# A linear-attention recurrence in half chunks of 64 tokens, stacked on the partitions

## The chip, the cores and the metric

The kernel runs on one NeuronCore of a Trainium2 chip. The metric is the device time of one execution in microseconds; the kernel before took 582.66 us (median of 3 runs, 580.79 to 582.68). The execution that was profiled took 582.26 us, of which the profile's span, from the first to the last instruction, is 580.3 us. All data are fp32 on the chip; the two weight matrices arrive as 64-bit floats and are converted there.

## What is computed

The reference is a gated linear recurrence (RWKV6, "Finch") followed by a two-layer block with a hard-swish gate. Cut to what matters:

```python
# r, k, v, w: (B=4, H=8, S=768, D=48); u: (H, D)
for t in range(S):
    cur = einsum('bhd,bhe->bhde', u * k[t], v[t])
    y[t] = einsum('bhd,bhde->bhe', r[t], state + cur)
    state = w[t][..., None] * state + einsum('bhd,bhe->bhde', k[t], v[t])
x = y.transpose(0, 2, 1, 3).reshape(3072, 384)
h = x @ w_in                       # 384 x 2048
out = (h * clip(h + 3, 0, 6) / 6) @ w_out   # 2048 x 384
```

For a piece of the sequence the recurrence becomes matrix products. With the decays multiplied up along the piece, r and k are scaled (called R and K below). The products K^T R, masked to the part above the diagonal, are the weights with which earlier tokens of the piece enter later ones; u gives the diagonal; the state from before the piece is read with R; and K^T v, added to the decayed state, is the next state.

## The kernel before, in words

**Tiling.** The 3072 tokens are 24 chunks of L = 128. Two sequences run side by side: chunks i and i+1 belong to different sequences, and chunk i continues chunk i-2. Chunks 0, 1, 12 and 13 are the first of their sequences. Eight heads of 48 are four pairs (P = 4): one head of a pair (g = 0) lies on partitions 0 to 47, the other (g = 1) on 64 to 111. Four chunks make a block of 512 tokens (BC = 4), which goes through the two big matrix products; there are six blocks (NB = 6).

**Steps of a chunk**, with the function and its engine:

- back_scan and fore_scan (L355, L364, VectorE) multiply the decays up along the tokens, backwards into E and forwards into W; make_k and make_r (L375, L379) scale k in place in E and r in place in W. They run on VectorE for chunks below EARLY, later on GpSimd. least (L382, ScalarE) saves the chunk's whole decay.
- own and own_sum give the diagonal u·r·k. For chunks below BY_PE it is one product on VectorE (L388) and four small matmuls (own_dot, L398); later two products on GpSimd from r and k laid out by token (L391, L392) and a reduction on VectorE (L406). diagonal (L414, ScalarE) spreads it over A, eight copies of the identity scaled by one column each.
- score (L422): for each pair two matmuls of 48 rows, 128 columns of weights and 128 moving columns, on the upper and the lower half of the array's rows. above (L429, VectorE) puts the part above the diagonal into A.
- turn_k (L438) and turned_k (L443): K turned so that tokens lie on the partitions.
- read: read_state (L474) multiplies the decayed state S with R; write (L484) computes K^T v; read_values (L491) multiplies v with A. State and values add up in one PSUM tile, y_ps. leave (L544, L545, ScalarE) copies it out into xT and, for the last pair of heads, into x3; last_pair moves x3 into xT by DMA.
- new_state (L448, L450, VectorE) adds the decayed state and K^T v; decay (L455) multiplies the state by the next chunk's whole decay.

In block 0 the last pair of heads can't wait for the DMA: read_last, leave_last and read_rest spread it by a matmul with a selection matrix (L521).

**Block work.** Block 0 uses the plain products (up L577, down L596) for its first half and the seven-product scheme for the rest; blocks 1 to 5 use that scheme throughout, which forms two-by-two products with seven instead of eight multiplications (up_product L678, down_product L729, with sums on VectorE and evacuation on ScalarE and VectorE).

**Order.** Nothing is ordered by hand. plan.add gives each step an engine, an estimate of its length, what it comes after, a due time (the key) and the buffers it holds; Plan.order walks through them and emits, for each engine, the step with the lowest key among those that can start. Each engine then runs its list in order. The due times of the recurrence follow from BASE (when a block starts) minus LAG; START, CONV, UP and SUMS are due times of the first stage, in which the weights are converted (fetch, low, whole, shift, join, full). Up to the first up product, spare time on TensorE is filled with matmuls on the identity (spin, L1047; ten of them are sets of four small ones, L1044).

Of the kernel before, what the change touches and what calls it, by code (L numbers as in the profile page):

```python
# [18 lines left out]
L = 128  # L19
GP = 64  # L20
# [6 lines left out]
LAG = 12.5  # L27
BEHIND = (-1, -1, -1, 0, 6, 7)
BY_PE = 4
OWN = 0.5  # L30
EARLY = 3
START = (-119.6, -152.0, -58.6, -43.4, 14.5, 25.8)
CONV = (-91.7, 6.6)
UP = (-83.9, 4.3, -71.3, 4.8)
SUMS = (53.5, 2.3)
# [148 lines left out]
def fast_path(tc, feat, tok, wflat, ub, ug, moe_w_in, moe_w_out, out, flag, n_chunks):  # L184
# [3 lines left out]

    nc = tc.nc
# [15 lines left out]
    with ExitStack() as ctx:  # L205
# [24 lines left out]
        mask = const.tile([128, L], U8, name="mask")  # L230
        back = const.tile([PR, P, L + 1], F32, name="back")
        starts = [const.tile([PR, P, L + 1], F32, name=f"start_{i}") for i in range(2)]
# [6 lines left out]
        def constants():  # L239

            nc.vector.memset(back, 0.0)
            nc.vector.memset(back[:, :, L:], 1.0)
            for b in starts:
# [3 lines left out]
            make_identity(nc, ident)  # L247

            mask_f = wk.tile([128, L], F32, name="clip")
            nc.gpsimd.memset(mask_f, 1.0)  # L250
            nc.gpsimd.affine_select(out=mask_f, in_=mask_f, compare_op=ALU.is_gt, fill=0.0, base=0,
                                    pattern=[[1, L]], channel_multiplier=-1)
            nc.gpsimd.tensor_copy(out=mask, in_=mask_f)

            x3_0 = blocks[0]["x3"] = wk.tile([PR, MB], F32, name="x3", bufs=1)
# [6 lines left out]


        n = P * L
        plan.ring("feat", 3)
        plan.ring("tok", 3)

        def load_feat(i):
            a = io.tile([PR, nf], F32, name="feat_in")
            if i == 0:  # L270
                nc.sync.dma_start(out=a[:, 2 * n:], in_=feat[chunk_of[i], :, 2 * n:])
                nc.scalar.dma_start(out=u_col, in_=ug)
            else:
                nc.sync.dma_start(out=a, in_=feat[chunk_of[i]])
            st[i].update(a=a, r=a[:, :n].rearrange("q (p t) -> q p t", p=P),
                         k=a[:, n:2 * n].rearrange("q (p t) -> q p t", p=P), w=a[:, 2 * n:])
# [7 lines left out]
        def load_tok(i):  # L284
            b = io.tile([L, 3, HD], F32, name="tok_in", bufs=3)
            if i < BY_PE:
                nc.sync.dma_start(out=b[:, 2], in_=tok[chunk_of[i], :, 2])
            else:
                nc.sync.dma_start(out=b.rearrange("s c e -> s (c e)"), in_=tok[chunk_of[i]].rearrange("s c e -> s (c e)"))
            st[i].update(rt=b[:, 0], kt=b[:, 1], v=b[:, 2].rearrange("s (h d) -> s h d", d=D))  # L290
# [55 lines left out]
        for r, k in (("E", 2), ("W", 2), ("rk", 1), ("dg", 2), ("A", 2), ("kn", 2), ("S", 2), ("x", 2), ("x3", 1), ("y", 1),  # L346
# [3 lines left out]
        w_min = const.tile([PR, NT, P], F32, name="w_min")  # L350

        def back_scan(i):
            d = st[i]
            E_ = wk.tile([PR, P * (L + 1)], F32, name="E", bufs=2)
# [3 lines left out]
            d["E"] = E_.rearrange("q (p t) -> q p t", p=P)  # L358
            nc.vector.reciprocal(out=starts[i % 2][:, :, 0:1], in_=d["E"][:, :, 0:1])

        def fore_scan(i):
            d = st[i]
            W_ = wk.tile([PR, P * (L + 1)], F32, name="W", bufs=2)
# [3 lines left out]
            d["R"] = W_.rearrange("q (p t) -> q p t", p=P)[:, :, :L]  # L367
# [4 lines left out]
        def make_k(i):  # L372
            d = st[i]
            d["K"] = d["E"][:, :, 1:]
            early(i).tensor_mul(d["K"], d["k"], d["K"])  # L375
# [8 lines left out]
        def own(i):  # L384
            d = st[i]
            if i < BY_PE:
                d["rk"] = wk.tile([PR, P, L], F32, name="rk", bufs=1)
                nc.vector.tensor_mul(d["rk"], d["r"], d["k"])  # L388
# [20 lines left out]
        def diagonal(i, x):  # L409
            d = st[i]  # L410
            if x == 0:
                d["A"] = wk.tile([L, H, L], F32, name="A")
            for h in range(x * H // 2, (x + 1) * H // 2):
                nc.scalar.activation(out=d["A"][:, h, :], in_=ident, func=ACT.Copy, scale=d["dg"][:, h])  # L414

        def score(i):
            d = st[i]
            d["a_ps"] = [pp.tile([128, P, L], F32, name="bankB"), pp.tile([128, P, L], F32, name="bankC", bufs=2)]
            for p in range(P):
                for g in range(2):  # L420
                    rows = slice(g * GP, g * GP + D)
                    nc.tensor.matmul(d["a_ps"][g][:, p, :], lhsT=d["K"][rows, p, :], rhs=d["R"][rows, p, :],  # L422
                                     start=True, stop=True)

        def above(i):

            d = st[i]
            for g in range(2):
                nc.vector.copy_predicated(  # L429
                    out=d["A"].rearrange("s (p g) t -> s g p t", g=2)[:, g],  # L430
                    mask=mask.rearrange("s (x t) -> s x t", x=1).to_broadcast([L, P, L]),
                    data=d["a_ps"][g])

        def turn_k(i):
            d = st[i]
            d["kn_ps"] = pp.tile([L, P, PR], F32, name="ps")
            for p in range(P):
                nc.tensor.transpose(d["kn_ps"][:, p, :], d["K"][:, p, :], ident[0:PR, 0:PR])  # L438

        def turned_k(i):  # L440
            d = st[i]
            d["kn"] = wk.tile([L, P, PR], F32, name="kn")
            nc.scalar.copy(out=d["kn"], in_=d["kn_ps"])  # L443

        def new_state(i):
            d = st[i]
            if is_first(i):
                nc.vector.tensor_copy(out=states[i % 2], in_=d["kv_ps"])  # L448
            else:
                nc.vector.tensor_add(states[i % 2], d["S"], d["kv_ps"])  # L450

        def decay(i):
            d = st[i]
            d["S"] = wk.tile([PR, P, D], F32, name="S")
            early(i).tensor_mul(d["S"], states[i % 2], d["E"][:, :, 0:1].to_broadcast([PR, P, D]))  # L455


        PLACES = ((0, 0), (0, 3), (1, 2), (1, 0))

        def into(i, p, g):  # L460
            d = st[i]
            bank, at = PLACES[p]
            rows = (g ^ bank) * GP
            fresh = (bank, rows) not in d["started"]
            d["started"].add((bank, rows))
            return dict(out=d["y_ps"][rows:rows + D, bank, at, :], start=fresh, skip_group_check=True)
# [919 lines left out]
```

## Time and profile before

| What | Value |
|---|---|
| Time, median of 3 | 582.66 us |
| Span of the profiled execution | 580.3 us |
| DVE (VectorE) busy | 408.7 us, 70% |
| ACT (ScalarE) busy | 265.7 us, 46% |
| POOL (GpSimd) busy | 120.4 us, 21% |
| First up product of block 0 (L577) starts | 31.01 us |
| First up product of block 1 (L678) starts | 147.60 us |
| Moved by DMA | 65.70 MB, mean 113 GB/s |

How to read it: the profile names the engines PE (TensorE matmuls), PEld (TensorE weight loads), DVE, ACT, POOL and SP (the queue that issues transfers). The page has the busy time of each, the same in 40 slices of the span, the DMA queues, the chain of waits that ended last (followed backwards from the last instruction, each step to what released it), the groups of instructions by source line, and the transfers. Besides the page, the trace answers questions: busy time by stretch, a timeline, who waited for whom. A matmul in fp32 shows as two records[...], with a weight load ahead of each.

### The profile page before, as it was taken

The numbers are of one execution on the slowest core, as the hardware profiler recorded it, in microseconds if no ns is written. First come the engines' busy times: TensorE is split into PE (matmuls) and PEld (weight loads), VectorE is DVE, ScalarE is ACT, GpSimd is POOL, SyncE is SP. The second block draws the span as 40 slices with busy tenths as digits, with TensorE's granted clock in tenths as the row PEclk, the third lists the DMA queues.
The fourth block names the chain that finished last, engine by engine and source line by source line (L and its number), as shares of the span: only waits on it lengthen the run. The fifth ranks groups of instructions, "written<-read, shape, count | busy, mean of one in ns | idle before, by whom it ended". The sixth has DMA issues, their size and how long they took to land.

```text
span 580.3 us, 10344 instructions
## 1 busy us (share of the span) xinstructions
PE 568.5 (98%) x4064; PEld 505.4 (87%) x4064; DVE 408.7 (70%) x674; ACT 265.7 (46%) x683; POOL 120.4 (21%) x114
## 2 busy tenths in 40 slices
PE   8999999999999999999999999999999999999995
PEld 7988677687888998888999888999988899988995
DVE  7799988898887877777967667967565625255350
ACT  2778773514756403467261277333266510255100
POOL 1003405425503023113152123031331000000000
PEclk7899999999999999999999999999999999999999
DMA  8979732524433454363245343254010000000001
GB/s 277 250 245 277 238 110 63 179 69 151 145 114 103 143 174 127 114 199 99 97 154 200 118 147 104 103 180 139 30 42 6 4 6 29 30 1 0 1 15 47
DMA packets 20906, 65.70 MB, mean 113 GB/s; under 512 B 2880, under 2 KB 7552, under 8 KB 20848
## 3 DMA queue, kind: packets, MB, share of 16 engines
q1 hardware_dynamic: 20720, 64.95, 35.3%
q8 instruction: 34, 0.56, 0.4%
q14 instruction: 24, 0.20, 0.1%
q10 hardware_dynamic: 128, 0.00, 0.0%
HBM read 59.24 MB, written 4.72 MB: 110 GB/s over the span
## 4 chain that ended last, share of the span: by engine, by line
PE 91%; DVE 7%; issue 1%; ACT 0%; POOL 0%; DVEq 0%; POOLq 0%
PE bankA L729 20%; PE bankA L678 18%; PE bankC L729 9%; PE bankC L678 9%; PE bankB L678 6%; PE bankB L729 5%; PE bankB L422 4%; PE y_ps L491 4%; PE bankA L596 3%; PE bankA L1047 2%; PE bankA L577 2%; PE bankC L577 2%; PE y_ps L474 2%; PE ps L484 2%; DVE top L337 1%; PE ps L438 1%
## 5 line engine op out<-in xcount | busy, mean ns | idle before, releaser
L687 ACT COPY g<-bankA 128x256 f32<-128x256 f32 x120 | 44.3, 371 | 61.3 <-PE bankA L678 59.3
L567 ACT ACTIVATE clip<-g,three 128x512 f32<-128x512 f32 x80 | 57.9, 724 | 12.9 <-DVE g L689 10.1
L729 PE MATMUL bankA<-w_out,g 128*128 128x192 f32 x352 | 62.5, 327 | 0.2 <-DVE w_out L650 0.2
L414 ACT ACTIVATE A<-ident,dg 128x128 f32<-128x128 f32 x192 | 59.4, 390 | 5.2 <-DVE dg L406 4.9
L678 PE MATMUL bankA<-xT,w_in 128*128 128x256 f32 x240 | 61.3, 381 | 0.0
L697 DVE SCALAR_TENSOR_TENSOR g<-clip,g 128x512 f32<-128x512 f32 x80 | 57.3, 721 | 5.2 <-ACT clip L567 4.7
L729 PEld LDWEIGHTS bankA<-w_out,g 128*128 128x128 f32 x352 | 57.9, 190 | 1.8 <-issue 0.8
L678 PEld LDWEIGHTS bankA<-xT,w_in 128*128 128x128 f32 x240 | 45.1, 190 | 6.6 <-issue 0.4
L379 POOL TENSOR_TENSOR W<-feat_in,W 112x512 f32<-112x512 f32 x21 | 27.6, 1313 | 108.6 <-DVE W L364 90.1
L742 ACT ACTIVATE o<-bankA 128x192 f32<-128x192 f32 x33 | 10.9, 331 | 80.6 <-PE bankA L729 80.6
L455 POOL TENSOR_TENSOR S<-state,E 112x192 f32<-112x192 f32 x19 | 18.0, 946 | 136.2 <-DVE state L450 59.1
L678 PE MATMUL bankB<-xT,w_in 128*128 128x256 f32 x160 | 41.1, 379 | 0.0
L375 POOL TENSOR_TENSOR E<-feat_in,E 112x512 f32<-112x512 f32 x21 | 27.4, 1304 | 64.9 <-ACT w_min L382 44.1
L544 ACT COPY xT<-y_ps 48x384 f32<-48x384 f32 x40 | 18.9, 473 | 43.3 <-PE y_ps L491 42.9
L689 DVE TENSOR_TENSOR g<-bankC,g 128x256 f32<-128x256 f32 x40 | 16.9, 422 | 26.8 <-PE bankC L678 23.9
L678 PEld LDWEIGHTS bankB<-xT,w_in 128*128 128x128 f32 x160 | 30.4, 190 | 4.1
L689 DVE TENSOR_TENSOR g<-bankB,g 128x256 f32<-128x256 f32 x40 | 17.0, 424 | 24.0 <-PE bankB L678 21.5
L355 DVE TENSOR_TENSOR_SCAN E<-feat_in,back 112x516 f32<-112x516 f32 x24 | 30.1, 1253 | 1.9 <-DMA feat_in<-in_feat_dram 1.7
L729 PE MATMUL bankA<-bits,g 128*128 128x192 f32 x176 | 30.7, 328 | 0.0
L729 PE MATMUL bankB<-w_out,g 128*128 128x192 f32 x176 | 30.6, 326 | 0.0
L364 DVE TENSOR_TENSOR_SCAN W<-feat_in,start 112x516 f32<-112x516 f32 x24 | 30.0, 1251 | 0.1
L422 PEld LDWEIGHTS bankB<-W,E 48*128 48x128 f32 x192 | 24.0, 193 | 6.6 <-issue 5.7
(273 smaller groups left out, 1265.6 us busy)
## 6 DMA issues: line engine op xcount, KB each, us to landing
feat_in<-in_feat_dram SPq DMA_DIRECT2D x23, 674.2 KB, 4.9
tok_in<-in_tok_dram SPq DMA_DIRECT2D x20, 576.0 KB, 3.8
bits<-in_moe_w_in_dram SPq DMA_DIRECT2D x8, 768.0 KB, 7.8
bits<-in_moe_w_out_dram SPq DMA_DIRECT2D x8, 768.0 KB, 5.3
feat_in<-in_moe_w_in_dram SPq DMA_DIRECT2D x8, 768.0 KB, 4.3
feat_in<-in_moe_w_out_dram SPq DMA_DIRECT2D x8, 768.0 KB, 4.3
out_dram<-o SPq DMA_DIRECT2D x24, 192.0 KB, 1.9
feat_in<-in_wflat_dram SPq DMA_DIRECT2D x6, 768.0 KB, 4.3
```

The source lines that it names most:

```text
L355: nc.vector.tensor_tensor_scan(out=E_[:, ::-1], data0=d["w"][:, :0:-1], data1=back.rearrange("q p t -> q (p t)")[:, ::-1], initial=0.0, op ...
L364: nc.vector.tensor_tensor_scan(out=W_, data0=d["w"][:, :-1], data1=starts[i % 2].rearrange("q p t -> q (p t)"), initial=0.0, op0=ALU.mult, ...
L375: early(i).tensor_mul(d["K"], d["k"], d["K"])
L379: early(i).tensor_mul(d["R"], d["r"], d["R"])
L414: nc.scalar.activation(out=d["A"][:, h, :], in_=ident, func=ACT.Copy, scale=d["dg"][:, h])
L422: nc.tensor.matmul(d["a_ps"][g][:, p, :], lhsT=d["K"][rows, p, :], rhs=d["R"][rows, p, :], start=True, stop=True)
L567: nc.scalar.activation(out=c[:, :m], in_=src, func=ACT.Relu, bias=three, scale=1.0)
L678: nc.tensor.matmul(b["p", q, to][:, :HB], lhsT=w, rhs=rhs, start=(n == 0 and k in (1, 2, 5)), stop=(n == len(terms) - 1 and k in (2, 3, 4) ...
L687: nc.scalar.copy(out=to, in_=src)
L689: nc.vector.tensor_add(to, src, to)
L697: nc.vector.scalar_tensor_tensor(out=g, in0=b["r", q, p], scalar=6.0, in1=g, op0=ALU.min, op1=ALU.mult)
L729: nc.tensor.matmul(b["d", p, to][:, :h], lhsT=a, rhs=w(), start=(f == 0 and k in (1, 2, 5)), stop=(f == HF - 1 and k in (2, 3, 4)), skip_g ...
```

## The change

A chunk stays 128 tokens for loads, turns and blocks, but the recurrence inside it runs in two halves of 64 tokens (HL = 64, index a). The half a of a chunk lies on partitions 64a to 64a+63 wherever tokens are on the partitions. So scores, values, state reads and writes are matmuls of at most 64 rows and 64 columns of weights, and (half, head) picks one of four quarters of the array. A state at the middle of the chunk is needed: decay gives the state for half 0, middle adds K^T v of half 0, decay_middle decays it for half 1, new_state adds K^T v of half 1. It is for leaving out the quarter of the scores and values that lies between the two halves, which the state carries instead, and for using all of the array.

What comes with it:

- A, mask and the identity for the diagonal are 64 columns wide (eyes); K gets a tile of its own instead of lying in E.
- K^T v (write) now goes into free columns of a y_ps tile, is copied out by ScalarE (written, kvs), and is computed two chunks ahead, inside read(i) for chunk i+2. For chunks 0, 2, 3, 4 and 5 (SOLO) it is a step of its own. The last chunks of a sequence, which had no write, now write their first half.
- From block 1 on read is split: begin(i) reads the state and turns K of chunk i+2; read(i) writes chunk i+2, multiplies the values of chunk i and computes the scores of chunk i+1. Where there is no write between the state read and the values, a drain of TensorE stands.
- x3 is part of the xT tile; r and k by token are loaded apart from v; BY_PE goes from 4 to 9, EARLY from 3 to 2, all spins are full matmuls, and the due times (LAG, START, CONV, UP, SUMS and the new AHEAD and LEAD) are set anew.

```diff
-LAG = 12.5
-BY_PE = 4
-EARLY = 3
-START = (-119.6, -152.0, -58.6, -43.4, 14.5, 25.8)
-CONV = (-91.7, 6.6)
-UP = (-83.9, 4.3, -71.3, 4.8)
+LAG = 7.2
+AHEAD = -14.5
+LEAD = 2.5
+BY_PE = 9
+SOLO = (0, 2, 3, 4, 5)
+EARLY = 2
+START = (-114.5, -137.4, -25.9, -60.3, 1.7, -1.3)
+CONV = (-95.3, 7.2)
+UP = (-48.5, 1.5, -30.7, 7.6)
...
         def score(i):
-            d["a_ps"] = [pp.tile([128, P, L], F32, name="bankB"), pp.tile([128, P, L], F32, name="bankC", bufs=2)]
+            d["a_ps"] = [pp.tile([128, P, HL], F32, name="bankB"), pp.tile([128, P, HL], F32, name="bankC", bufs=2)]
             for p in range(P):
-                for g in range(2):
-                    rows = slice(g * GP, g * GP + D)
-                    nc.tensor.matmul(d["a_ps"][g][:, p, :], lhsT=d["K"][rows, p, :], rhs=d["R"][rows, p, :],
-                                     start=True, stop=True)
+                for a in range(2):
+                    for g in range(2):
+                        rows = slice(g * GP, g * GP + D)
+                        nc.tensor.matmul(d["a_ps"][g][a * HL:(a + 1) * HL, p, :], lhsT=d["K"][rows, 2 * p + a, :],
+                                         rhs=d["R"][rows, 2 * p + a, :], start=True, stop=True)
...
+        def middle(i):
+            d = st[i]
+            nc.vector.tensor_add(d["S"][:, 1], d["S"][:, 0], d["kvs"][:, 0])
+        def decay_middle(i):
+            decayed(early(i), i, 1, st[i]["kvs"][:, 0] if is_first(i) else st[i]["S"][:, 1])
         def new_state(i):
-                nc.vector.tensor_add(states[i % 2], d["S"], d["kv_ps"])
+            nc.vector.tensor_add(states[i % 2], st[i]["S"][:, 1], st[i]["kvs"][:, 1])
...
         def read_values(i, pairs):
             for p in pairs:
-                for g in range(2):
-                    nc.tensor.matmul(lhsT=d["v"][:, 2 * p + g, :], rhs=d["A"][:, 2 * p + g, :], stop=True,
-                                     **into(i, p, g))
+                for a in range(2):
+                    for g in range(2):
+                        half = slice(a * HL, (a + 1) * HL)
+                        nc.tensor.matmul(lhsT=d["v"][half, 2 * p + g, :], rhs=d["A"][half, 2 * p + g, :], stop=True,
+                                         **into(i, a, p, g))
...
+        def begin(i):
+            new_y(i)
+            read_state(i, range(P))
+            if i + 2 < NT:
+                turn_k(i + 2)
         def read(i):
-            new_y(i)
-            read_state(i, (0, 2, 1, 3))
-            write(i)
+            if i + 2 < NT:
+                write(i + 2)
+            else:
+                nc.tensor.drain()
             read_values(i, range(P))
+            if i + 1 < NT:
+                score(i + 1)
```

## The prediction

> **What bounds the kernel now.** I read the page's first part, then the shares of the chain that ended last, then a table of busy time by stage, and last the timeline of TensorE inside one chunk.
>
> ```profile
> PE 568.5 (98%) x4064; PEld 505.4 (87%) x4064; DVE 408.7 (70%) x674; ACT 265.7 (46%) x683; POOL 120.4 (21%) x114
> ...
> PE 91%; DVE 7%; issue 1%; ACT 0%; POOL 0%; DVEq 0%; POOLq 0%
> ```
> TensorE is 98% busy and holds 91% of the chain; VectorE is the only other engine there. A busy share is a mean over stages, so I split it (columns: stretch, its length, then busy us of PE, PEld, DVE, ACT, POOL with record counts, granted clock, DMA share, GB/s):
>
> ```profile
> 0.00:31.00 31.00, 29.00 (x282) 25.45 (x283) 22.79 (x35) 14.99 (x37) 2.64 (x13) 0.83 0.91 262
> 31.00:75.00 44.00, 41.93 (x295) 33.84 (x294) 42.67 (x65) 33.70 (x72) 10.81 (x9) 1.00 0.80 254
> 75.00:118.00 43.00, 43.00 (x290) 31.73 (x289) 38.08 (x65) 24.36 (x63) 16.41 (x14) 1.00 0.34 106
> 118.00:147.60 29.60, 28.28 (x293) 25.15 (x291) 27.98 (x36) 9.77 (x32) 13.49 (x11) 1.00 0.34 106
> ...
> 190.00:350.00 160.00, 159.90 (x1145) 145.90 (x1144) 118.57 (x193) 69.64 (x191) 38.28 (x33) 1.00 0.44 143
> ```
> 147.60 is where block 1's first up product starts (L678 in the timeline). There are two regimes. After it TensorE alone is full (159.90 of 160.00) and VectorE has a quarter free: a microsecond off TensorE is a microsecond off the run. Before it both are full at once: from 31 to 75 us VectorE is busy 42.67 of 44.00 us. A saving on TensorE alone there buys little. The first 31 us hold the prelude.
>
> One steady chunk on TensorE (start, us, then what ran; each fp32 matmul leaves two records, a transpose one):
>
> ```profile
> 276.80 0.37 PE L422 MATMUL bankB<-W,E 48*128 48x128 f32 x1
> 276.81 0.37 PE L422 MATMUL bankC<-W,E 48*128 48x128 f32 x1
> ...
> 277.57 0.27 PE L422 MATMUL bankB<-W,E 48*128 48x128 f32 x1
> 277.58 0.27 PE L422 MATMUL bankC<-W,E 48*128 48x128 f32 x1
> 277.68 0.27 PE L422 MATMUL bankB<-W,E 48*128 48x128 f32 x1
> 277.69 0.27 PE L422 MATMUL bankC<-W,E 48*128 48x128 f32 x1
> 277.89 1.13 PE L678 MATMUL bankA<-xT,w_in 128*128 128x256 f32 x4
> ...
> 288.02 0.66 PE L474 MATMUL y_ps<-W,S 48*48 48x128 f32 x16
> 288.61 0.61 PE L484 MATMUL ps<-tok_in,kn 128*64 128x48 f32 x15
> 289.01 0.30 PE L491 MATMUL y_ps<-A,tok_in 128*48 128x128 f32 x1
> 289.05 0.22 PE L484 MATMUL ps<-tok_in,kn 128*64 128x48 f32 x1
> 289.11 1.04 PE L491 MATMUL y_ps<-A,tok_in 128*48 128x128 f32 x15
> 290.07 1.24 PE L729 MATMUL bankA<-w_out,g 128*128 128x192 f32 x6
> ```
> Durations of records overlap, so path time is start to next start. The two row halves start 0.01 apart: they run together. A round of all tiles then takes 0.11 us (277.57 to 277.68) for 128 moving columns. The scores take 277.89 - 276.80 = 1.09 us, of which 8 rounds are 0.87 and 0.22 is entering and leaving the tiled mode. The state read takes 0.59, the write 0.40, the values 289.01 to 290.07 = 1.06. The four turns took 0.44 (263.79 to 264.23).
>
> [...] L474 uses four quarters, and its 16 records in 0.59 us are 4 rounds of 0.11 plus some 0.15 for the change. [...] 16 records on two column halves take 0.45 (288.61 to 289.05 for the last 64-column record, then about one round), so a round is 0.055 to 0.06[...]. [...] The trace shows starts 0.01 apart inside a round, but no long run with more than one record per 24 ns; the new shapes need one per 14.5 ns.
>
> **The change, part by part.** Chunks stay 128 tokens, but each is two halves of 64 with a state in between. Counts below are of the program's issue order.
>
> *Scores:* 8 matmuls (48 rows, 128x128) become 16 (64x64), four at once: 32 records / 4 = 8 rounds. A round is bound by a 64-column stream (half of 0.11)[...]: I take 0.058. 0.87 becomes 0.46. *Values:* likewise, 0.87 becomes 0.46. *State read:* twice the matmuls at half the columns: 0.44 becomes 8 x 0.058 = 0.46. *Write:* 0.40 becomes 0.46[...]. *Turn:* 0.44, unchanged.
> *Order:* write of i+2, values of i, and scores of i+1 follow each other in one mode; state read goes with the turn of i+2 into a separate begin. Excursions stay at two a chunk; overhead was 0.22 + (2.05 - 0.44 - 0.40 - 0.87 = 0.34) and becomes some 0.22 + 0.25.
>
> *TensorE after 147.6.* Before, 15 scores, 15 values, 13 state reads, 11 writes and 11 turns are left: 15 x 1.09 + 15 x 0.87 + 13 x 0.44 + 11 x 0.40 + 11 x 0.44 + 15 x 0.34 = 49.5 us. After, from the same landmark, 14 scores, 15 values, 14 state reads, 11.5 writes (last chunks now write their first half) and 13 turns: (14 + 15 + 14 + 11.5) x 0.46 + 13 x 0.44 + 14 x 0.22 + 15 x 0.25 = 37.6. **Saved 12.0**, all on the path.
>
> *TensorE from 31 to 147.6.* Seven chunks give back some 5 us, but five more chunks take own_dot (L398, 0.81 each from 44.31 to 45.12: +4.1), five solo writes add 0.2 of mode change each, the selection of the third head doubles its loads (+0.6 a chunk, two chunks), and one more score, 1.5 writes and two turns lie ahead of the landmark: net about +2.
>
> *VectorE up to the same place.* Predicated copies halve (0.62 to some 0.35 each, 18: -4.8); five reductions go (0.54: -2.7); K and R of chunk 2 move to GpSimd (-1.4); added are five own products (0.68: +3.4), eight middle adds (L450's 0.34: +2.8), two early decays less one (+0.4), one state more (+0.3), one back and two fore scans that are ahead of their time (+3.9). Net +2 on 131.5. Both engines are level, so the stage stays as it was, unless the prelude gives something.
>
> *Prelude.* The clock was halved from 8.6 to 18.8 us (0.50 in the same table cut there). The ten four-tile spins before that gap are full-array ones now; if the clock holds, half-speed turns, dots and spins shrink and up products could start 3 us earlier. On the other side chunks 0 and 1 now need write, copy, decay before their first read. I count 0, with -3.5 to +2.
>
> *Costs at nothing.* ScalarE: state copies (kvs, about 0.5 as L443) against eight diagonal copies of half the columns; it is 42% busy after 147.6. GpSimd: a second decay (L455, 0.95) against five chunks' products gone; 18% busy after 147.6. DMA: five token loads shrink from 576 to 192 KB, 1.9 MB less early on. New waits: begin waits for decay_middle, and behind it on TensorE queues everything; its chain, write to copy to add to decay, is about 0.5 + 0.34 + 0.95 plus hops, 2.5 us, and is issued two chunks (some 35 us) ahead, so up and down products cover it. The last chunk of each block is read at least 9.7 us of TensorE work ahead of the next block's first product, against about 7.5 for leave (1.5), moves (1.8 + 2.2) and sums (1.7).
>
> Sum: 582.66 - 12.0 + 0 = **570.7 us**.
>
> **Rivals.**
> *Issue-bound quarters (slower).* If a record costs 25 ns, a group of 32 takes 0.80, +0.34. After 147.6: 54.5 groups, +18.5; before it 30.5 groups, +10.4, part of it under VectorE, say 7.5. 570.7 + 26 = 596.7. For it: nothing in the trace sustains the rate. Against: loads and starts in a round come 0.01 apart.
> *VectorE keeps the first stage longer.* The first up products come in a row while conversions are queued ahead of their gates; TensorE in order then waits. A slip of 6 us: 576.7. For it: 97% busy there.
> *Better start.* Clock held (-3.5) and rounds at 0.055 (-1.3): 565.9.
> *Begin waits.* 0.8 us of wait at each of 15 begins eats the gain: 582.7, no change.
>
> **Numbers.** Forecast 0.58, better start 0.13, VectorE 0.13, issue-bound 0.10, begin waits 0.06. Range 564.5 to 580: from the better start to the VectorE case with 3 us more; left out are the issue-bound case and the waits, 0.16. Faster: the first three, 0.84. The waits split into 0.04 same and 0.02 slower; with the issue-bound case slower is 0.12.
>
> **What would show it.** Rounds of scores and values 0.055 to 0.06 apart and each of these groups near 0.46 confirm the core; 0.10 breaks it. Block 1's first up product near 147.6; later is the VectorE case. From there to the end about 420.7 instead of 432.7 us. No wait on the y tiles at begin. What would make me wrong: an uncounted serialisation between quarters that add into the same rows, or ScalarE late with kvs.

## The result and the profile after

The changed kernel takes 579.67 us (median of 4 runs, 579.48 to 580.76), against 582.53 us for the kernel before on the same chip: a ratio of 0.9962, interval [0.9939, 0.9984]. It is faster by 0.4%, where 2% was forecast. The span of the profiled execution went from 580.33 to 578.06 us.

First the page's busy times and the shares of the chain that ended last, of the kernel after:

```profile
PE 557.9 (97%) x5622; PEld 500.2 (87%) x5622; DVE 405.4 (70%) x693; ACT 275.5 (48%) x724; POOL 130.1 (23%) x131
...
PE 87%; DVE 7%; DMA 2%; issue 1%; ACT 1%; SPq 0%; DVEq 0%
```

TensorE's busy time fell from 568.5 to 557.9 us, by 10.6. The forecast was 10 (12.0 saved after block 1's start, 2 added ahead of it). So TensorE's work is near the forecast (the table below splits it), but the span is shorter by only 2.3. TensorE is now not busy for 20.1 us of the span; it was 11.9. In the chain the share of TensorE fell from 91% to 87%.

Where that idle time lies is seen in busy time by stretch, of the kernel after (stretch, its length, busy us of PE, PEld, DVE, ACT, POOL with record counts, granted clock, DMA share, GB/s). The stretches are cut where block 0's first up product (30.96) and block 1's (158.7) start:

```profile
30.96:75.00 44.04, 36.10 (x332) 28.88 (x332) 36.94 (x57) 30.20 (x63) 8.67 (x7) 0.88 0.70 213
...
118.00:158.70 40.70, 38.62 (x632) 33.70 (x630) 34.92 (x54) 18.21 (x57) 23.37 (x20) 1.00 0.36 105
...
190.00:350.00 160.00, 160.00 (x1725) 147.36 (x1724) 120.56 (x203) 77.11 (x217) 44.81 (x45) 1.00 0.47 147
```

In the steady part TensorE is full, as it was (160.00 of 160.00). The prelude ends at the same place. From 30.96 to 75 TensorE is busy only 36.10 of 44.04 us, where it had 41.93 of 44.00, and its clock was 0.88 instead of 1.00. The first stage, from block 0's first up product to block 1's, in the same view, first before and then after:

```profile
31.01:147.60 116.59, 113.19 (x874) 90.70 (x872) 108.72 (x164) 67.83 (x166) 40.71 (x33) 1.00 0.51 162
```

```profile
30.96:158.73 127.77, 117.10 (x1455) 95.01 (x1454) 107.67 (x170) 72.79 (x187) 45.83 (x38) 0.96 0.46 139
```

| us | before | after | difference |
|---|---|---|---|
| Block 0's first up product starts | 31.01 | 30.96 | -0.1 |
| Block 1's first up product starts | 147.60 | 158.73 | **+11.1** |
| From there to the end of the span | 432.72 | 419.34 | **-13.4** |
| First stage, whole | 116.59 | 127.77 | **+11.2** |
| First stage: TensorE busy | 113.19 | 117.10 | +3.9 |
| First stage: TensorE idle | 3.40 | 10.67 | +7.3 |
| First stage: VectorE busy | 108.72 | 107.67 | -1.1 |

The gain after block 1's start is larger than forecast. The first stage, forecast to stay as it was, takes 11.2 us longer and takes most of the gain away.

The waits of TensorE on other engines, of the kernel after (engine, tile and line, what ended the wait: us in total, times, longest), name the main one:

```profile
PE bankC L639 <- DVE g L650: 5.7, 2, 5.4
PE ps L415 <- DVE rk L405: 1.6, 1, 1.6
...
PE bankB L791 <- DVE A L447: 1.3, 1, 1.3
```

The timeline of TensorE around it (start, us, then what ran; in brackets the idle time before it and what ended it; four up products and a turn lie ahead of it, from 30.96 on):

```profile
37.52 0.67 PE L536 MATMUL y_ps<-v_in,kn 64*64 64x48 f32 x32 [0.75 <-ACT kn L461]
39.79 1.02 PE L415 MATMUL ps<-u_col,rk 112*128 112x2 f32 x8 [1.59 <-DVE rk L405]
46.16 2.93 PE L639 MATMUL bankC<-xT,w_in 128*128 128x256 f32 x6 [5.35 <-DVE g L650]
...
49.63 2.13 PE L639 MATMUL bankA<-xT,w_in 128*128 128x256 f32 x6
```

Before this four up products of block 0 ran in a row. The fifth (46.16) needs the bank of PSUM (the memory that TensorE writes its results to) that the first filled, and that bank comes free when VectorE has gated it (L650): the 5.35 us of idle time end with that gate. The same up product with the same shapes then takes 2.93 us instead of 1.46. What VectorE did meanwhile, in its own timeline:

```profile
39.56 0.55 DVE L349 TENSOR_SCALAR top<-bits 128x768 int32<-128x768 int32 x1
40.15 1.82 DVE L354 SCALAR_TENSOR_TENSOR top<-bits,top 128x768 int32<-128x768 int32 x1
42.10 1.71 DVE L359 CUSTOM_DVE_ANT_0 w_in<-top,more 128x1536 uint16<-128x1536 uint16 x1
...
45.70 0.41 DVE L650 SCALAR_TENSOR_TENSOR g<-clip,bankC 128x256 f32<-128x256 f32 x1
...
46.36 0.95 DVE L359 CUSTOM_DVE_ANT_0 w_in<-top,more 128x1536 uint16<-128x1536 uint16 x1
...
48.48 0.96 DVE L354 SCALAR_TENSOR_TENSOR top<-bits,top 128x768 int32<-128x768 int32 x1
```

Up to that gate it is never idle: after the product for the diagonal (38.98) five conversion steps of the weights (39.56, 40.15, 42.10, 43.74, 44.63) stand ahead of the first gate in its list. Two of them, 1.82 and 1.71 us, take nearly twice what they take a little later (0.96 and 0.95). And the clock, cut to stretches:

```profile
37.30:40.70 3.40, 1.58 (x40) 1.49 (x40) 3.37 (x5) 3.01 (x5) 1.56 (x1) 1.00 0.72 220
...
40.80:46.16 5.36, 0.01 (x1) 0.00 (x0) 5.19 (x6) 2.93 (x11) 4.16 (x4) 0.50 0.60 203
46.16:51.00 4.84, 4.83 (x14) 3.92 (x15) 3.42 (x7) 3.36 (x6) 0.00 (x0) 0.51 1.02 330
...
47.50:50.90 3.40, 3.40 (x11) 2.71 (x11) 1.98 (x5) 2.02 (x4) 0.00 (x0) 0.50 1.03 339
```

TensorE's clock is halved from 40.7 to 50.9 us. The first half of that costs nothing, since TensorE waits; in the second it works 4.83 us at 0.51, which by my estimate (half of that, as the same matmuls take about twice as long) is about 2.4 us of work lost. So of the 3.9 us that TensorE is busier in the first stage about 1.5 are more work. The half clock lasted 10.2 us and began as the long wait did (the last record ahead of it ends at 40.81). TensorE was busy for all of its last 3.4 us. In the 3.4 us before it TensorE was not idle: its records fill 1.58 us, and the wait of 1.59 us (up to 39.79) lies among them. What sets its start and its end is not shown by this trace.

Last the steady chunk, TensorE's timeline of the kernel after, first the group that is read and then begin:

```profile
277.84 0.62 PE L536 MATMUL y_ps<-v_in,kn 64*64 64x48 f32 x30
278.24 0.25 PE L523 MATMUL y_ps<-A,v_in 64*48 64x64 f32 x2
...
278.72 0.24 PE L440 MATMUL bankB<-W,K 48*64 48x64 f32 x1
...
279.21 0.22 PE L440 MATMUL bankC<-W,K 48*64 48x64 f32 x1
279.36 1.35 PE L740 MATMUL bankA<-xT,w_in 128*128 128x256 f32 x5
```

```profile
289.93 0.67 PE L514 MATMUL y_ps<-W,S 48*48 48x64 f32 x32
290.53 0.60 PE L456 MATMUL ps<-ident,K 112*128 112x112 f32 x4
```

The write starts at 277.84, the values at 278.24, the scores at 278.72, and their last record at 279.21: 0.40, 0.48 and about 0.5 us where the forecast had 0.46 for each. 32 records in 0.48 us are one every 15 ns, and a round of four every 0.06. State read and turn take 0.60 and 0.44 (the next down product, not shown, starts at 290.97), with no wait in front.

### The profile page after: what moved, and what is told of

It reads as the page before. It is cut to its first block, busy times and chain, and to the rows that moved or that the text cites. A ratio compares the mean times of both kernels' runs of the same rounds, so it can differ in the third digit from the quotient of the medians.

```text
span 578.1 us, 13556 instructions
## 1 busy us (share of the span) xinstructions
PE 557.9 (97%) x5622; PEld 500.2 (87%) x5622; DVE 405.4 (70%) x693; ACT 275.5 (48%) x724; POOL 130.1 (23%) x131
## 4 chain that ended last, share of the span: by engine, by line
PE 87%; DVE 7%; DMA 2%; issue 1%; ACT 1%; SPq 0%; DVEq 0%
PE bankA L791 19%; PE bankA L740 18%; PE bankC L791 9%; PE bankC L740 9%; PE bankB L740 6%; PE bankB L791 5%; PE bankA L658 3%; PE bankA L639 3%; PE bankC L639 3%; PE y_ps L514 2%; PE y_ps L523 2%; PE y_ps L536 2%; PE ps L456 2%; DVE E L372 2%; DMA feat_in<-in_feat_dram 1%; PE bankB L440 1%
## 5 line engine op out<-in xcount | busy, mean ns | idle before, releaser
L759 DVE SCALAR_TENSOR_TENSOR g<-clip,g 128x512 f32<-128x512 f32 x80 | 56.0, 704 | 6.5 <-ACT clip L629 6.4
L396 POOL TENSOR_TENSOR W<-feat_in,W 112x512 f32<-112x512 f32 x22 | 32.6, 1483 | 80.4 <-DVE W L381 80.4
L431 ACT ACTIVATE A<-eyes,dg 128x64 f32<-128x64 f32 x192 | 49.3, 336 | 0.6 <-DVE dg L423 0.2
L469 POOL TENSOR_TENSOR S<-S,w_min 112x192 f32<-112x192 f32 x20 | 20.8, 1041 | 115.2 <-DVE S L477 108.5
L392 POOL TENSOR_TENSOR K<-feat_in,E 112x512 f32<-112x512 f32 x22 | 27.6, 1255 | 72.2 <-DVE E L372 37.4
L606 ACT COPY xT<-y_ps 48x256 f32<-48x256 f32 x80 | 29.3, 367 | 26.2 <-PE y_ps L523 25.2
L372 DVE TENSOR_TENSOR_SCAN E<-feat_in,back 112x520 f32<-112x520 f32 x24 | 33.1, 1379 | 5.3 <-DMA feat_in<-in_feat_dram 5.3
L381 DVE TENSOR_TENSOR_SCAN W<-feat_in,start 112x520 f32<-112x520 f32 x24 | 31.9, 1331 | 1.5 <-PE y_ps L514 1.1
L639 PE MATMUL bankC<-xT,w_in 128*128 128x256 f32 x96 | 25.2, 401 | 5.7 <-DVE g L650 5.7
```

The costliest lines, as they stand in the source:

```text
L372: nc.vector.tensor_tensor_scan(out=E_[:, ::-1], data0=d["w"][:, :0:-1], data1=back.rearrange("q p t -> q (p t)")[:, ::-1], initial=0.0, op ...
L381: nc.vector.tensor_tensor_scan(out=W_, data0=d["w"][:, :-1], data1=starts[i % 2].rearrange("q p t -> q (p t)"), initial=0.0, op0=ALU.mult, ...
L396: early(i).tensor_mul(d["R"], d["r"], d["R"])
L431: nc.scalar.activation(out=d["A"][:, h, :], in_=eyes, func=ACT.Copy, scale=d["dg"][:, h])
L606: nc.scalar.copy(out=blocks[bk]["xT"][g * GP:g * GP + D, :, at:at + HL], in_=st[i]["y_ps"][(g ^ a) * GP:(g ^ a) * GP + D, a, :, :])
L639: nc.tensor.matmul(h_ps[:, :(c1 - c0) * L], lhsT=w_in[:, f // 2, j, f % 2, :], rhs=b["xT"][:, j, c0 * L:c1 * L], start=(j == 0), stop=(j = ...
```

## The experiments

In this table every time is in us. The ratio is to the kernel before, measured beside it on the same chip; times of different rows are best compared by it. Block 0 and block 1 are the starts of their first up products in the profiled execution, and the rest runs from block 1 to the end of the span.

| Kernel | Time | Ratio, interval | Block 0 | Block 1 | Rest |
|---|---|---|---|---|---|
| before | 582.53 | 1 | 31.01 | 147.60 | 432.72 |
| after | 579.67 | 0.9962 [0.9939, 0.9984] | 30.96 | 158.73 | 419.34 |
| e5_turns | 610.47 | 1.0534 [1.0463, 1.0606] | 32.60 | 169.10 | 440.32 |
| e2_gates | 582.02 | 1.0008 [0.9995, 1.0022] | 30.25 | 154.12 | 425.08 |
| e1_warm | 592.83 | 1.0200 [1.0172, 1.0228] | 29.06 | 168.88 | 419.45 |
| e7_warm2 | 577.23 | 0.9927 [0.9903, 0.9951] | 30.66 | 156.08 | 420.36 |
| e3_after_nojoin | 575.41 | 0.9912 [0.9884, 0.9939] | 30.23 | 154.05 | 419.65 |
| e4_before_nojoin | 579.14 | 0.9964 [0.9952, 0.9976] | 32.02 | 145.21 | 431.86 |
| e8_after_noconv | 570.34 | 0.9806 [0.9783, 0.9828] | 29.90 | 148.40 | 420.41 |
| e9_before_noconv | 578.39 | 0.9947 [0.9932, 0.9962] | 31.92 | 145.73 | 431.38 |
| e6_bype4 | 587.93 | 1.0109 [1.0090, 1.0128] | 30.18 | 165.49 | 419.57 |
| e10_both | 585.29 | 1.0074 [1.0048, 1.0100] | 29.10 | 163.20 | 419.16 |
| e11_early3 | 581.42 | 0.9983 [0.9968, 0.9997] | 30.85 | 160.57 | 419.52 |
| e12_early3_warm | 586.32 | 1.0066 [1.0039, 1.0093] | 29.74 | 161.69 | 418.89 |

Block 0 doesn't start at the same time even where nothing ahead of it was changed: e1_warm and e7_warm2 are the changed kernel up to there, and start it at 29.06 and 30.66, against 30.96. So a shift of block 1 by 1 or 2 us can come from the prelude of the one execution that was profiled, and the first stage is the difference of the two columns.

The theory after the result: the mechanism on TensorE holds, and the gain is lost in the first stage, by waits on VectorE and by the half clock that begins with the long one, at 40.7 us, and outlasts it by 4.7. Its rivals: the order of VectorE's list alone is at fault; or TensorE's added work is.

### Is it the four quarters that make the recurrence shorter?

```diff
 def score(i):
...
-    for p in range(P):
-        for a in range(2):
-            for g in range(2):
+    for a in range(2):
+        for g in range(2):
+            for p in range(P):
```

The same turn of the loops in read_values. Four matmuls in a row now use the same quarter of the array; the work is the same.

> The changed kernel with the loops of score and read_values turned, so that four matmuls in a row use the same quarter of the array before the next quarter comes; the same 16 matmuls each, the same results. Theory A (four quarters work at once only while neighbours in the queue use different ones, since TensorE starts in order): a group of scores or values goes from about 0.46 us towards 4 x 0.46 = 1.8 us; 48 such groups cost 0.6 to 1.3 us more each, total 608 to 640. Theory B (TensorE runs far enough ahead in its queue to keep the quarters busy in any order): within 2 us of the changed kernel, about 0.4% under before.

The time rose by 5% and is above that of the kernel before. The rest after block 1 is 21.0 us longer. TensorE's timeline of this kernel, inside a steady chunk (the scores, which follow the values from 295.22 on, are left out):

```profile
293.69 0.68 PE L536 MATMUL y_ps<-v_in,kn 64*64 64x48 f32 x32
294.19 1.24 PE L523 MATMUL y_ps<-A,v_in 64*48 64x64 f32 x29
```

The write, whose loops are unchanged, takes 0.50 (293.69 to 294.19) where it took 0.40. The values take from 294.19 to about 295.2, where they took 0.48. 29 groups of scores and values lie after block 1's start, so 21.0 / 29 = 0.72 us more for each, about 1.2 us a group. That is still less than the 1.8 us that the expectation gives for no overlap at all. So the gain on TensorE is the overlap of quarters, and most of it is lost when neighbours in the queue use the same quarter.

### Is it the order in which VectorE gates?

```diff
-plan.add(f"ramp{n_}", "ACT", ..., k - 3, ...)
+plan.add(f"ramp{n_}", "ACT", ..., k - 25 * (x == 0) - 3, ...)
-plan.add(f"gate{n_}", "DVE", ..., k - 3, ...)
+plan.add(f"gate{n_}", "DVE", ..., k - 25 * (x == 0) - 3, ...)
```

The gates of block 0's first half get due times 25 us earlier, so that they go ahead of conversions.

> The changed kernel with the due times of ramp and gate in the first half of block 0 brought forward by 25 us, so that on VectorE and ScalarE they stand ahead of the later weight conversions instead of behind them. Theory A (the loss in the first stage is one misplaced order: up product f=4 waits 5.35 us for a gate queued behind conversions): the wait goes and with it the halved clock, block 1 starts at 150 to 153, total 571 to 574. Theory B (VectorE and the conversions set the pace, and the wait only moves): TensorE waits as long elsewhere, for conversions or masks; block 1 at 157 or later, total 578 to 582.

The wait of 5.35 us is gone, and the time is that of the kernel before (its interval contains 1). TensorE now runs eight up products in a row and then waits elsewhere. From its waits in this kernel:

```profile
PE y_ps L584 <- ACT xT L576: 2.0, 1, 2.0
PE bankA L658 <- DVE w_out L359: 1.9, 3, 0.9
```

The converted weight of L359 is one of the steps that the gates overtook, and the product for the diagonal (L405, 1.8 us of wait in the same list) is another. The clock halves again, and this time TensorE works through most of it (the first column behind the length is its busy time):

```profile
64.60:74.80 10.20, 9.30 (x68) 6.71 (x69) 9.62 (x12) 7.14 (x17) 1.51 (x1) 0.50 0.70 218
```

Half of 9.30 us, about 4.7 us by the same estimate, is lost here, against 2.4 in the changed kernel. TensorE's idle time in the first stage did fall, from 10.67 to 8.68 us. Block 1 starts 4.6 us earlier, but the rest is 5.7 us longer: more work was left for behind it (512 records of values against 480, and more of the other steps), so a time at a landmark must be read together with what follows it. One new order moves the wait, and takes away only part of it. That doesn't prove that no order would, and this one was not run with the clock held.

### What does the half clock cost?

```diff
+def warm(n):
+    for _ in range(n):
+        nc.tensor.matmul(bank("bankB")[:, :L], lhsT=ident, rhs=ident, start=True, stop=True)
...
 def own_dot(i):
...
+    if i == 3:
+        warm(6)
...
 def write_alone(i):
+    if i == 2:
+        warm(3)
...
 def up(f, c0, c1):
...
+    if f == 4 and c0 == 0:
+        warm(22)
```

31 matmuls on the identity in the three idle places ahead of the fifth up product.

> The changed kernel with extra matmuls on the identity (3 before the lone write of chunk 2, 6 before the diagonal product of chunk 3, 22 before the first-half up product f=4), 31 in all, 6.7 us at full clock, placed where TensorE stood idle for 7.7 us; the order of all else is unchanged. Theory A (the halved clock from 40.9 to 51.1 us, which follows the waits, is a loss of its own): the clock stays at 1.00, the ten up products after the wait run at 1.29 instead of up to 2.7 us, block 1 starts 2.5 to 3 us earlier (about 156), total about 577. Theory B (VectorE sets the pace of the first stage, whatever TensorE's clock): block 1 stays within 1 us of 158.7, total 579 to 580.5.

This experiment missed its aim. TensorE's timeline of this kernel:

```profile
40.60 17.47 PE L413 MATMUL bankB<-ident 128*128 128x128 f32 x44
```

Each extra matmul took a new PSUM tile of the same bank and so, as I read it, waited for the one before: 6 took 3.06 us in the second place (36.73 to 39.79), 22 took some 17.3 in the third. So the first stage grew by about 12 us. It says nothing on the cost of the half clock, so I mended it: one tile for each place, with start on its first matmul and stop on its last.

```diff
 def warm(n):
-    for _ in range(n):
-        nc.tensor.matmul(bank("bankB")[:, :L], lhsT=ident, rhs=ident, start=True, stop=True)
+    b = bank("bankB")
+    for x in range(n):
+        nc.tensor.matmul(b[:, :L], lhsT=ident, rhs=ident, start=(x == 0), stop=(x == n - 1))
```

> As e1_warm, but the extra matmuls of one place all go into one bank allocated once, so that none waits for the one before: 31 matmuls of about 0.22 us, 6.7 us, in the idle 7.7 us ahead of up product f=4. Theory A (the halved clock after the wait is a loss of its own): clock 1.00 from 10 us on, block 1 at 155.5 to 156.5, total 2 to 3 us under the changed kernel (ratio to before about 0.991 to 0.993). Theory B (VectorE sets the pace): the up products that ran slowly now wait instead; ratio 0.995 to 0.998.

TensorE's timeline of the mended kernel at the same place:

```profile
40.31 5.16 PE L414 MATMUL bankB<-ident 128*128 128x128 f32 x44
45.87 1.56 PE L650 MATMUL bankC<-xT,w_in 128*128 128x256 f32 x6 [0.40 <-DVE g L661]
```

The clock stays full up to the last microsecond (1.00 in every stretch from 30.66 to 156.1 us, and 1.00 as the mean of the span). Only the tile and the flags of its first and last matmul were changed, and 22 matmuls take 5.16 instead of 17.47 us, which bears the reading out. The fifth up product starts at 45.87 instead of 46.16, since it waits for the same gate, but takes 1.56 instead of 2.93 us. The first stage is 2.4 us shorter than in the changed kernel, which is what the estimate above gave for the half clock; the rest is 1.0 us longer. The ratios 0.9927 and 0.9962 put the difference of the whole at 2.0 us, but their intervals overlap. So the half clock's part of the first stage is seen in the profile, and that it costs about 2 us in all is likely and not certain.

### Does the gain come when VectorE has less to do?

Both kernels, before and after, with one VectorE operation of every pair of weight tiles left out (the join, L354 and L337):

```diff
-plan.add(f"join{j}", "DVE", 0.96, do(high_join, j), ...)
+plan.add(f"join{j}", "DVE", 0.96, lambda: None, ...)
```

> The changed kernel without the step that joins the sign to the converted weights (L354, 16 times about 1.0 us on VectorE, all in the first stage); signs are left out of the weights, nothing else, and the order is unchanged. Theory B (VectorE sets the pace of the first stage): block 1 starts 8 to 12 us earlier (147 to 151), total 568 to 572. Theory A (a misplaced order): only what the joins ahead of the first gate held up comes back, up to 5.35 us of wait and 2.5 us of halved clock; block 1 at 151 to 154, total 572 to 575. If neither: within 2 us of 579.7.

> The kernel before without the same joining step (signs left out of the weights), as the control. TensorE there has 3.4 us of waits between its first up product and block 1, so at most that can come back: 579 to 581.5 under both theories, if the prelude stays at 31 us. A gain above 5 us would say that VectorE already held the kernel before.

Some 16 us less on VectorE in either (page: 405.4 to 389.1, and 408.7 to 392.3). By the ratios the changed kernel gains 0.5% by it and the one before 0.4%, so the difference between the two grows by less than the intervals are wide. In the changed kernel the wait for the gate falls from 5.35 to 2.99 us, the half clock from 10.2 to 6.8 us, and TensorE's idle time in the first stage from 10.67 to 6.98 us; in the one before that idle time falls too, from 3.40 to 0.48. So VectorE's load costs TensorE waits in both kernels, but the first stage of the changed one is still 10.6 us longer (123.82 and 113.19). That doesn't decide for the theory. So the next pair leaves out nearly all of the conversion, on VectorE and on ScalarE: one VectorE operation for a pair of weight tiles stays, which writes the tile.

```diff
-c["top"] = wk.tile([128, 2 * DM], I32, name="top")
-nc.vector.tensor_scalar(out=c["top"], in0=c["hi"], ...)
+nc.vector.tensor_scalar(out=c["dst"].rearrange("p a b e -> p (a b e)"), in0=c["hi"], ...)
...
-plan.add(f"low{j}", "ACT", 0.9, do(low_scaled, j), ...)
-plan.add(f"whole{j}", "ACT", 0.84, do(low_whole, j), ...)
+plan.add(f"low{j}", "ACT", 0.9, lambda: None, ...)
+plan.add(f"whole{j}", "ACT", 0.84, lambda: None, ...)
...
-plan.add(f"join{j}", "DVE", 0.96, do(high_join, j), ...)
-plan.add(f"full{j}", "DVE", 0.94, do(high_low, j), ...)
+plan.add(f"join{j}", "DVE", 0.96, lambda: None, ...)
+plan.add(f"full{j}", "DVE", 0.94, lambda: None, ...)
```

> The changed kernel with the weight conversion cut to one VectorE operation per pair of weight tiles (the shift, written straight to the weights, 0.56 us); low_scaled, low_whole, high_join and high_low are left out, about 31 us off VectorE and 28 us off ScalarE, all in the first stage; the weights are then wrong numbers, the order of all else is unchanged. Theory B (the shorter recurrence on TensorE is worth its 10.5 us, and the loaded engines beside it in the first stage hand 8.3 us of it back as waits): with them relieved, TensorE's idle time in the first stage falls below that of a relieved kernel before plus 2 us, and the total is 8 to 12 us under e9_before_noconv, 567 to 571. Theory A' (the waits are the new recurrence's own latency, write to copy to add to decay, and the order written for it): the gap to e9_before_noconv stays at 2 to 4 us, 573 to 576.

> The kernel before with the conversion cut in the same way, as the control of e8_after_noconv. Its TensorE idles 3.4 us between its first up product and block 1 and little in the prelude, so 577 to 580 under both theories.

The first stage in these two, busy time by stretch, first the changed kernel's variant:

```profile
29.90:148.40 118.50, 114.63 (x1454) 93.29 (x1453) 80.01 (x142) 51.87 (x161) 42.60 (x38) 1.00 0.53 148
```

then that of the kernel before:

```profile
31.92:145.73 113.81, 112.44 (x874) 90.68 (x872) 77.98 (x135) 48.08 (x140) 45.95 (x33) 1.00 0.51 162
```

With VectorE at 80.01 of 118.50 us TensorE idles 3.87 us there instead of 10.67, at full clock. The first stage is 4.7 us longer than in the variant of before, where it was 11.2 longer with the conversions, and the rest is 11.0 us shorter. The difference of the two variants is 578.39 - 570.34 = 8.05 us (8.3 by the two profiled spans). Of those 8.3 us 2.0 lie ahead of block 0 (29.90 against 31.92), where the two executions differ, and can't be put down to the recurrence by this. From block 0 on the shorter recurrence is worth 6.3 us where VectorE and ScalarE have room, and 2.2 (11.2 lost, 13.4 gained) where they have not. In this pair every step keeps its place, a left-out step only does nothing; so it is the work in the lists that brings most of the waits, in an order that stays the same. The pair takes work off both engines and doesn't tell which of the two it was that mattered. The waits of the changed kernel, on gates for the most part, speak for VectorE.

### Is it TensorE's added work?

```diff
-BY_PE = 9
+BY_PE = 4
```

> The changed kernel with BY_PE back at 4, so the diagonal of chunks 4 to 8 comes from GpSimd and a reduction on VectorE (the way of the kernel before) and no longer from a VectorE product and four small matmuls on TensorE. The term at stake is the five own_dot (0.69 us each measured, 3.5 us of TensorE path in the first stage). Theory A, TensorE's own work counts one for one in the first stage: block 1 starts 3 to 4 us earlier (about 155 us) and the time falls to about 576. Theory B, the first stage is set by the order and load of VectorE: VectorE loses five products (0.68 each) but gains five reductions (0.54 each), so block 1 stays within 1.5 us of 158.7 and the time within 1.5 us of 579.7. The rest after block 1 stays near 419.5 in both.

> The same edit (BY_PE 4) together with 31 extra identity matmuls in the idle places of TensorE ahead of the fifth up product, which alone gave 577.2 us. If the two gains are independent, theory A gives 577.2 - 3.5 = about 573.7; theory B about 577. Clock at full throughout in both; if the idle places move with the edit, part of the extra matmuls becomes work on the path and the time is up to 2 us more.

Both theories were wrong: the edit made the kernel about 8 us slower, with the extra matmuls and without (in e10_both, too, the clock halves, for 10.2 and for 6.8 us). From TensorE's waits in e6_bype4:

```profile
PE y_ps L514 <- ACT kvs L543: 4.3, 3, 1.8
```

The old wait for the gate is still there (5.2 us in the same list). This one is new: three state reads wait for the copied K^T v. GpSimd is busy 15.53 us between 30.96 and 75, where it had 8.67, in part with the products that own_dot had spared it, and the planner orders the chunks around them differently. Two of these waits (71.0 and 85.8) are followed by half clock, and TensorE works through it:

```profile
73.90:80.70 6.80, 6.66 (x57) 3.88 (x56) 6.42 (x10) 5.05 (x15) 0.28 (x1) 0.50 0.96 325
...
87.60:94.40 6.80, 6.67 (x64) 4.98 (x64) 4.83 (x7) 2.66 (x11) 2.41 (x2) 0.50 0.12 31
```

By the estimate used above that is 6.7 us lost, most of the 8. So the five own_dot, which the prediction counted as +4.1 us on TensorE, do cost about 3.5 us there (own_dot takes 1.69 us in the first stage of the kernel before and 5.15 in the changed one, start to next start), but with them in place the changed kernel is spared these waits and their half clock.

### Is it GpSimd, beside VectorE?

In the changed kernel GpSimd works on K, R and the decays of chunk 2 from 34.42 to 36.0 and from 39.14 to 44.97 us, where it idled until 48.07 before (EARLY went from 3 to 2). That is just where VectorE's conversion steps took 1.82 and 1.71 us. GpSimd's timeline of the changed kernel:

```profile
34.42 1.58 POOL L392 TENSOR_TENSOR K<-feat_in,E 112x512 f32<-112x512 f32 x1 [7.01 <-PE bankA L639]
39.14 3.86 POOL L396 TENSOR_TENSOR W<-feat_in,W 112x512 f32<-112x512 f32 x2 [3.14 <-DVE W L381]
42.97 2.00 POOL L469 TENSOR_TENSOR S<-state,w_min 112x192 f32<-112x192 f32 x2
```

```diff
-EARLY = 2
+EARLY = 3
```

> The changed kernel with EARLY back at 3: K, R and the decays of chunk 2 on VectorE instead of GpSimd. In the changed kernel's trace GpSimd works from 34.4 to 36.0 and from 39.1 to 45.0 us on them, just when two VectorE conversion steps take 1.82 and 1.71 us instead of 0.96 and TensorE waits 5.35 us for the gate behind them; the kernel before has GpSimd idle until 48 us. Theory C, GpSimd slows VectorE there: the three stretched steps fall back to about 0.96 each (2.5 us off VectorE) but K, R and decays cost VectorE about 0.7 + 0.7 + 0.3 x 2 = 2.0 more, partly at other places; the wait shrinks to 3 to 4 us, block 1 at 156 to 158, time 577 to 579. Theory A/B, VectorE's load in the stage as such sets it: no gain or up to 1 us slower, wait 5 us or more.

> The same edit with the 31 extra identity matmuls that hold TensorE's clock (alone 577.2 us). If EARLY 3 helps by itself it gives some 575.5 to 576.5 here; if VectorE's load sets the stage, 577 to 578. The clock is to stay full throughout.

VectorE's and then GpSimd's timeline in e11_early3:

```profile
35.61 1.82 DVE L354 SCALAR_TENSOR_TENSOR top<-bits,top 128x768 int32<-128x768 int32 x1
...
39.11 0.96 DVE L354 SCALAR_TENSOR_TENSOR top<-bits,top 128x768 int32<-128x768 int32 x1
```

```profile
35.20 1.41 POOL L396 TENSOR_TENSOR W<-feat_in,W 112x512 f32<-112x512 f32 x1 [3.71 <-DVE W L381]
36.57 1.22 POOL L469 TENSOR_TENSOR S<-state,w_min 112x192 f32<-112x192 f32 x1
```

The join takes 1.82 beside GpSimd and 0.96 without it, so the stretching is real: by these pairs of lines GpSimd's work holds such a step up. By what means is not shown. Not every step is held up: the one at 39.56 takes its usual 0.55 beside GpSimd. The wait at the fifth up product fell to 3.65 us, and the one of 1.59 for rk is gone. But no time came back: the median is 1 to 2 us higher, with intervals that overlap. TensorE waits 1.39 for a converted weight at 64 us, 0.65 twice for xT and 1.46 for kvs, and the clock halves again, here too with TensorE at work all the time:

```profile
79.00:85.80 6.80, 6.80 (x18) 4.96 (x18) 5.03 (x5) 3.17 (x12) 2.20 (x2) 0.50 0.45 131
```

That alone is 3.4 us lost by the estimate. With the extra matmuls it was worse than e7_warm2 by 1.4%, against either expectation; the execution that was profiled, 4 us faster than the median of that kernel, has new waits of 2.62 and 1.81 us, and its clock halves for 3.4 us. Theory C is right on what stretches VectorE and wrong on what that is worth: this cause, too, can be taken away and the time doesn't come back.

## Why the prediction was right or wrong

**Scores, values, writes, state reads: right.** The groups were forecast at 0.46 us and measured 0.40 to 0.5. Summed by kind from block 1's start on (start to next start of TensorE's records) scores went from 16.4 to 8.3 us, values from 15.2 to 7.4, state reads from 7.6 to 9.0, writes from 5.1 to 5.8 and turns from 4.7 to 5.7: 49.0 became 36.2, where the forecast had 49.5 and 37.6. From block 1's start to the end the gain is 13.4, not 12.0 (the forecast's own terms give 11.8); 12.8 of it is this sum, and TensorE's idle time there fell from 6.4 to 5.7 us.

**Issue-bound quarters: refuted.** 15 ns a record for 32 records in a row (0.48 us), and not 25, the pace of the write's 16 records in the kernel before (0.40 us).

**Begin waits: refuted.** No wait on y_ps at begin (L514) in the changed kernel's list.

**Prelude: right by luck.** TensorE did run at full clock early, as the better start had it. (The clock column can't show it, it reads 1.00 from the start; but the records of the identity matmuls start 0.21 us apart up to 6.5 us and 0.11 apart after that.) But VectorE's back scan of chunk 1 waited for its data and started at 10.31 instead of 8.88 us, and TensorE waited 1.38 us for v_in, so the first up product starts at 30.96. The two cancelled, as far as is seen, in this execution; in e1_warm, with the same prelude, block 0 starts at 29.06.

**VectorE's own work: right.** +2 on 131.5 was forecast; the view by stretch has 25.55 (to 30.96), 36.94, 35.77 (75 to 118) and 34.92 up to block 1, 133.2 in sum.

**TensorE's own work in the first stage: near, but not by its sum.** The terms that the forecast lists come to about +3.5 us (5 given back; 4.1, 1.0 and 1.2 added, and 2.2 for the score, the writes and the turns at its own prices), and not to the "about +2" that it writes. Measured are +3.9, and about 1.5 without the estimated loss to the half clock.

**The step that failed: "Both engines are level, so the stage stays as it was".** Its term was 0 and it measured +11.2 us: 7.3 of idle time, about 2.4 of half clock and about 1.5 of work. A near-equal sum of work did not show the waits between two engines that are both full. VectorE kept its amount of work but had it in another order, with conversions ahead of the gates, and slowed by GpSimd beside it (1.82 and 1.71 us for steps of 0.96 and 0.95); how much of the 7.3 us each of these brought is not shown. They were seen in part: conversions ahead of gates are the words of the rival "VectorE keeps the first stage longer", which gave 576.7 with a slip of 6 us and had a chance of 0.13. It was the nearest case. Its size was short, by 1.3 us of waits, the half clock and the work. That e7_warm2, with the clock held, comes to 577.2 is in part luck: in its profile the first stage is 8.8 us longer than before, not 6, and the profiled execution took 578.18. The clock was in my reading of the prelude alone, and I didn't carry it to a wait of 5 us. That K and R of chunk 2 go to GpSimd was booked as 1.4 us off VectorE and not as work that stretches VectorE's steps beside it.

**What stays open.** No single wait was found to carry the loss. Taking away the gate's wait (e2_gates), the own_dot (e6_bype4) or GpSimd's part (e11_early3) brought other waits, and half clock on stretches in which TensorE worked; taking work off VectorE and ScalarE (e8 against e9) brought 6.5 of the 11.2 us back. Which of the two engines it was, and how much of the 7.3 us a better order could regain at full load, was not found. The edits of e2_gates, e6_bype4 and e11_early3 let the planner order everything anew, so none of them changes one thing alone.

## What to carry to other kernels

Split a saving by stage, and where a second engine is as full as the first, price its waits and not its sum: here 10.6 us less of TensorE's busy time became 2.9 us. Ask of every wait of TensorE what its clock does next: the wait of 5.35 us here was paid twice, once waiting and once at half clock (0.51 for the 4.84 us behind it), and in e2_gates and e6_bype4 the half clock cost more than in the changed kernel. Matmuls without a wait among them, put into the gap, kept the clock full (1.00 in e7_warm2) and probably took back about 2 us. And give small matmuls on quarters of the array an order in which neighbours in the queue use different quarters: the other order cost 5% of the whole time.

## What the hardware showed that I had not expected

- 32 fp32 records of 64x64 quarters ran at one every 15 ns where four quarters alternate (the values, 278.24 to 278.72 us).
- Half clock lasted about 3.4 us or a multiple of it: 10.2 in the changed kernel, 6.8 in e3_after_nojoin, 3.4, 3.4 and 6.8 in e11_early3.
- The busy share of TensorE's records didn't tell whether the clock would hold. In the 3.4 us before the clock halved the records fill 1.58 us in the changed kernel, but 3.02 in e11_early3 (75.6 to 79.0).
- Matmuls that waited for one another didn't hold the clock. In e1_warm the clock was halved from 42.7 to 59.7 us, although the stretch (same columns as above) reads 15.96 of 17.00 us:

```profile
42.70:59.70 17.00, 15.96 (x42) 10.58 (x42) 4.77 (x8) 3.50 (x7) 0.35 (x1) 0.50 0.83 255
```

In e7_warm2 the same matmuls without these waits kept it at 1.00.
